# One transfer instead of two for each query and key tile of the first batch

## The chip, the cores and the metric

The kernel runs on 1 core of one Trainium2 chip. The metric is the device time of one execution in microseconds; lower is better. Three parts of that core matter here besides its matrix engine TensorE (PE): VectorE (DVE), ScalarE (ACT) and GpSimd (POOL), which do the elementwise work, SyncE (SP), whose queue issues almost every DMA, and the 16 DMA engines that carry out what it issues.

## What the kernel computes

Attention over `q`, `k`, `v` of shape 4 batches x 8 heads x 576 tokens x 64, then a dense layer with softplus, then a layer with one of eight experts per token.

```python
# attention: two parts, added
q_d = q.reshape(B, H, S // 4, 4, D).mean(axis=3)      # k_d, v_d alike
out_d = softmax_attention(q_d, k_d, v_d)               # 144 x 144 per head
mask = abs(pos[:, None] - pos[None, :]) < 4            # a band of 7 keys
out_local = softmax_attention(q, k, v, mask)
x = repeat(out_d, 4, axis=2) + out_local               # -> 2304 x 512
# dense layer
h = x @ w_in; g = softplus(h); x = g @ w_out           # 512 -> 2048 -> 512, weights in float64
# experts
e = argmax(x @ w_gate + modality_bias[id]); out = gate * (relu(x @ w1[e]) @ w2[e])
```

## The kernel before, in words

Attention works on pairs of heads: 16 pairs, four for each of four batches. The queue of work is a list of jobs. A `Down` job of a pair loads its queries, keys and values, brings queries and keys into the layout "two heads x 64 features on 128 partitions, tokens along the row" (`qT`, `kT`) and does the downsampled attention. Three `Local` jobs of the same pair do the band, 192 tokens each. Every job has six steps (`st_T`, `st_S`, `st_E`, `st_N`, `st_Ta`, `st_PV`), spread over successive steps of the queue (`pieces`), so that several jobs are under way at once. The first 19 steps of the queue run ahead of everything else; from then on the attention pieces are dealt out between the matrix products of the dense layer. At the same time the float64 weights of that layer are loaded (`raw`) and turned into float32 by DVE and ACT (`from_f64`, L439 to L443). The dense layer goes through six blocks of 384 tokens; block 0 needs the local attention of all four pairs of batch 0.

The tile framework fixes the order of the instructions on each engine when the program is built. It takes them in program order and by priority, against a timeline that it simulates, so an instruction whose assumed duration changes can move others.

The change touches how the first batch's queries and keys arrive. In batch 0 (`PE_TRANSPOSED = 1`) a tile `qr` or `kr` holds 96 partitions; partition p has tokens 6p to 6p+5 (`RT = 6`) of both heads. The tile of before is ordered token, head, feature, and each head is loaded by a DMA of its own (L135); what one DMA writes in a partition is six separate rows of 64 floats, 256 bytes each. `trans` (L162) then takes each of the six token slots, a block of 96 x 128 that holds both heads, through TensorE as a transposition against the identity (L172), three slots to a PSUM tile `pT`, and copies the PSUM tile to `qT` or `kT` with DVE or ACT (L177). Batches 1 to 3 use other loads (L139) and a transposition on DVE (L166), which the change leaves alone. On SP's queue each pair's loads stand in the order `qr`, `qr`, `kr`, `kr`, `vr` (L144), and `lv` (L291, values of the band) and `raw` (L456, L460) come between pairs. `qr` and `kr` of batch 0 share two buffers each (tags `wis`, `wos`), so the loads of pair 2 wait for the transpositions of pair 0.

The sums over four tokens (`sum4`, L188 and L185), the scores (L210, L311), the exponentials (L225, L325), the normalizing (L232, L331), the second transpositions (L239, L336) and the products with the values (L248, L344) follow from `qT` and `kT`. `warm` (L264) puts one idle product behind some steps.

Of the kernel before, what the change touches and what calls it, by code (L numbers as in the profile page):

```python
# [9 lines left out]
F32 = mybir.dt.float32  # L10
# [8 lines left out]
B, H, S, D = 4, 8, 576, 64  # L19
# [15 lines left out]
RT = 6  # L35
RP = S // RT
NBLK = S // 32
# [18 lines left out]
def band_attention__softplus_mlp__top1_moe(  # L56
# [14 lines left out]
    nc = tc.nc  # L71
    V, A, G, T = nc.vector, nc.scalar, nc.gpsimd, nc.tensor
# [8 lines left out]
    ident = const.tile([128, 128], F32, name="ident")  # L81
# [19 lines left out]
    mlp = ctx.enter_context(tc.tile_pool(name="mlp", bufs=2))  # L101
# [19 lines left out]
    class Down:  # L121
# [3 lines left out]
        def load(self):  # L125
            b, h0 = self.b, 2 * self.hp
            self.raw = []
            for src, nm in ((q, "qr"), (k, "kr")):
                tag = {"qr": "wis", "kr": "wos"}[nm] if b == 0 else "raw"
                on_pe = b < PE_TRANSPOSED  # L130
                t = mlp.tile([RP, RT, 2, D] if on_pe else [128, NBLK, 32], F32, tag=tag, name=nm,
                             bufs=RAWB if tag == "raw" else 2)
                for h in range(2):
                    if on_pe:
                        nc.sync.dma_start(out=t[:, :, h, :], in_=src[b, h0 + h].rearrange("(p r) d -> p r d", r=RT))  # L135
                        continue
                    for c in range(2):
                        p0 = h * D + c * 32
                        nc.sync.dma_start(  # L139
                            out=t[p0:p0 + 32],  # L140
                            in_=src[b, h0 + h, :, c * 32:(c + 1) * 32].rearrange("(n t) d -> t n d", t=32))
                self.raw.append(t)
            t = mlp.tile([SDH, 2, 2, FACTOR, D], F32, tag="raw", name="vr", bufs=RAWB)
            nc.sync.dma_start(  # L144
                out=t.rearrange("p h a r d -> p (h a) (r d)"),
                in_=v[b, h0:h0 + 2].rearrange("h (a p r) d -> p (h a) (r d)", a=2, p=SDH, r=FACTOR),
            )
            self.raw.append(t)
# [13 lines left out]
        def trans(self, i):  # L162

            t = apool.tile([128, S], F32, tag=("qT", "kT")[i], name="qkT", bufs=4)
            if self.b >= PE_TRANSPOSED:
                V.transpose(t, self.raw[i].rearrange("p n d -> p (n d)"))  # L166
                return t
            half = RT // 2
            for g in range(2):
                ps = pa("pT")  # L170
                for r in range(half):
                    T.transpose(ps[:, r * RP:(r + 1) * RP], self.raw[i][:, g * half + r].rearrange("p h d -> p (h d)"),  # L172
                                ident[:RP, :RP])
                warm(ps)
                o = t.rearrange("m (p r) -> m r p", r=RT)[:, g * half:(g + 1) * half, :]
                x = ps[:, :half * RP].rearrange("m (r p) -> m r p", r=half)
                (A.copy if i or g else V.tensor_copy)(o, x)  # L177
            return t
# [81 lines left out]
    def warm(ps):  # L260

        if 4 <= nloc[0] < 12:
            for i in range(1):
                T.matmul(ps[:, 384:384 + 128], ident, ident[:, :128], start=True, stop=True)  # L264

    def pa(name):

        if not started[0]:
            nps[0] += 1
            if nps[0] % 2:  # L270
                return psy.tile([128, 512], F32, tag="py", name=name)
        return psa.tile([128, 512], F32, tag="pa", name=name)
# [554 lines left out]
    if 0:  # L827
        ps = pa("pW")
# [169 lines left out]
    p, q, pos_q = stages[-1]  # L998
# [57 lines left out]
```

## Time and profile before

| | |
|---|---|
| median of 3 runs | 785.83 us (784.47 to 790.5) |
| the profiled execution's own time | 786.35 us |
| its span, first to last instruction | 784.5 us |
| PE busy | 749.1 us (95%) |
| DVE, ACT, POOL busy | 504.8, 461.2, 449.9 us |
| mean granted TensorE clock | 0.987 |

The profiled execution takes 1.85 us more than its span, and 0.52 us more than the median. The busy time of PE is nearly the whole span, but it is a mean over stages that differ: the early stages, where the change lies, have to be read by themselves.

### The profile page before, as it was taken

To read this page: it belongs to the slowest core of one execution; us is meant where nothing else is said; L and a number is where in the kernel's file an instruction comes from. 1 tells how busy PE (TensorE), PEld (TensorE's weight loads), DVE (VectorE), ACT (ScalarE), POOL (GpSimd) and SP (SyncE) were. 2 spreads that over 40 slices of the span, in tenths; PEclk is the share of its full clock that TensorE was granted. 3 is DMA by queue.
4 is the path that set the end of the run, shared out by engine and by line. 5 is a ranking of instruction groups with operands and counts; after the bars stand their busy time and mean duration, and the time that the engine had idled before them with its cause. 6 is when DMAs were issued, how large, how long until landed. Compare 5 with 4: busy or idle time off the path is not lost.

```text
span 784.5 us, 13833 instructions
## 1 busy us (share of the span) xinstructions
PE 749.1 (95%) x4917; PEld 657.3 (84%) x4918; DVE 504.8 (64%) x1067; ACT 461.2 (59%) x1204; POOL 449.9 (57%) x447
## 2 busy tenths in 40 slices
PE   6977999899999999999999999999999999999995
PEld 5754656579899989899899999999998889889884
DVE  6888999856764567976654555445996394274322
ACT  5835666667676646667565756555865365355432
POOL 3446322757765566766556556565769365455632
PEclk9987999999999999999999999999999999999999
DMA  8769666415000241311000100071002012001002
GB/s 190 175 138 270 194 196 188 77 26 119 23 13 15 71 83 28 72 24 52 1 13 13 52 1 2 1 271 65 1 21 101 21 61 82 0 1 68 14 0 85
DMA packets 111447, 55.46 MB, mean 71 GB/s; under 512 B 89593, under 2 KB 102411, under 8 KB 111371
## 3 DMA queue, kind: packets, MB, share of 16 engines
q1 hardware_dynamic: 111083, 53.98, 25.7%
q8 instruction: 41, 0.67, 0.4%
q10 hardware_dynamic: 288, 0.52, 0.2%
q14 instruction: 35, 0.29, 0.1%
HBM read 45.05 MB, written 9.44 MB: 69 GB/s over the span
## 4 chain that ended last, share of the span: by engine, by line
PE 75%; DVE 14%; DMA 3%; issue 2%; ACT 2%; SPq 2%; POOL 2%; DVEq 0%; ACTq 0%
PE py L623 22%; PE ph L582 20%; PE py L940 11%; PE ph L784 10%; DVE cva L442 2%; PE pS L311 2%; PE pO L344 2%; DMA qr<-in_q_dram 2%; PE ph L579 2%; DVE cva L440 2%; PE pA L336 2%; PE pS L210 1%; DVE cva L441 1%; PE pO L248 1%; DVE wi L443 1%
## 5 line engine op out<-in xcount | busy, mean ns | idle before, releaser
L623 PE MATMUL py<-g,wos 128*128 128x384 f32 x1056 | 212.5, 342 | 2.4 <-POOL g L606 1.1
L623 PEld LDWEIGHTS py<-g,wos 128*128 128x128 f32 x1056 | 181.7, 188 | 9.0 <-issue 3.0
L582 PE MATMUL ph<-xT,wis 128*128 128x384 f32 x960 | 183.1, 338 | 0.0
L582 PEld LDWEIGHTS ph<-xT,wis 128*128 128x128 f32 x960 | 166.6, 188 | 1.6 <-issue 0.4
L479 POOL TENSOR_TENSOR wis<-wi,wis 128x512 fp32r<-128x512 f32 x80 | 104.4, 1305 | 72.6 <-ACT wis L478 66.7
L479 POOL TENSOR_TENSOR wos<-wo,wos 128x512 fp32r<-128x512 f32 x88 | 117.8, 1339 | 47.5 <-ACT wos L478 47.4
L588 ACT ACTIVATE ga<-ph 128x384 f32<-128x384 f32 x96 | 46.9, 489 | 77.9 <-PE ph L582 74.9
L604 DVE SCALAR_TENSOR_TENSOR ph<-ph,ga 128x384 f32<-128x384 f32 x80 | 44.7, 560 | 49.4 <-ACT ga L590 49.4
L784 PE MATMUL ph<-xs,ws 128*128 128x384 f32 x378 | 73.9, 336 | 1.2 <-DVE u L789 1.2
L478 ACT CAST wos<-wo 128x512 fp32r<-128x512 f32 x88 | 54.3, 617 | 30.8 <-PE py L623 26.3
L784 PEld LDWEIGHTS ph<-xs,ws 128*128 128x128 f32 x378 | 67.1, 188 | 4.8 <-DVE u L789 1.6
L789 DVE TENSOR_TENSOR u<-ph,u 128x384 f32<-128x384 f32 x60 | 33.3, 555 | 58.6 <-PE ph L784 58.2
L940 PE MATMUL py<-wos,gs 128*128 128x512 f32 x270 | 69.0, 394 | 0.7 <-POOL gs L795 0.4
L325 ACT ACTIVATE ls<-ls,lst 128x70 f32<-128x70 f32 x144 | 49.4, 344 | 25.5 <-DVE lst L319 16.1
L940 PEld LDWEIGHTS py<-wos,gs 128*128 128x128 f32 x270 | 50.0, 188 | 9.9 <-POOL gs L795 0.8
L479 POOL TENSOR_TENSOR wos<-w2s,wos 128x512 fp32r<-128x512 f32 x24 | 33.5, 1395 | 34.3 <-ACT wos L478 34.3
L331 POOL TENSOR_TENSOR ls<-ls,lst 128x210 f32<-128x210 f32 x48 | 28.8, 601 | 42.2 <-DVE lst L330 15.5
L590 ACT ACTIVATE ga<-ga 128x384 f32<-128x384 f32 x96 | 50.2, 524 | 1.7
L589 ACT ACTIVATE ga<-ga 128x384 f32<-128x384 f32 x96 | 50.4, 525 | 0.4
L478 ACT CAST wis<-wi 128x512 fp32r<-128x512 f32 x80 | 48.9, 612 | 0.1
L579 PE MATMUL ph<-xN,wi 128*128 128x384 f32 x128 | 45.7, 499 | 1.2 <-DVE xf L360 1.1
L605 DVE CAST g<-ph 128x384 fp32r<-128x384 f32 x80 | 44.1, 552 | 4.2 <-PE py L623 1.1
(166 smaller groups left out, 1283.1 us busy)
## 6 DMA issues: line engine op xcount, KB each, us to landing
raw<-in_moe_w_in_dram SPq DMA_DIRECT2D x16, 512.0 KB
raw<-in_moe_w_out_dram SPq DMA_DIRECT2D x16, 512.0 KB
lv<-in_v_dram SPq DMA_DIRECT2D x72, 70.0 KB
vr<-in_v_dram SPq DMA_DIRECT2D x16, 288.0 KB
ydram<-y SPq DMA_DIRECT2D x12, 384.0 KB
yb<-ydram SPq DMA_DIRECT2D x12, 384.0 KB
out_dram<-ob SPq DMA_DIRECT2D x16, 256.0 KB
qr<-in_q_dram SPq DMA_DIRECT2D x48, 72.0 KB
```

The lines of the kernel that those rows point to most:

```text
L325: A.activation(s[:, i, :], s[:, i, :], AF.Exp, bias=st[:, 0, i], accum_out=st[:, 1, i])
L478: A.copy(w[:, 0], src)
L479: G.tensor_tensor(out=w[:, 1], in0=src, in1=w[:, 0].bitcast(F32), op=ALU.subtract)
L579: T.matmul(ps[:, :TB], wi[:, c, cc, :], xT[n][:, cc, :], start=(cc == 0), stop=(cc == CC - 1))
L582: T.matmul(ps[:, :TB], wt[:, w, cc, :], xT[n][:, x, cc, :], start=(i == 0), stop=(i == 3 * CC - 1))
L588: A.activation(a, ps[:, :TB], AF.Abs)
L589: A.activation(a, a, AF.Exp, scale=-1.0)
L590: A.activation(a, a, AF.Ln, bias=1.0)
L604: V.scalar_tensor_tensor(o, ps[:, :TB], 0.0, a, ALU.max, ALU.add)
L623: T.matmul(yps[n][dc][:, :TB], w[:, a, dsl], g[:, b, :], start=(c == 0 and i == 0), stop=(c == NC1 - 1 and i == 2))
L784: T.matmul(ps[:, :TB], ops[:, w, a, cc, :], xop[p, x][:, l, cc, :], start=i == 0, stop=i == 5)
L940: T.matmul(yps[n][t], g[:, a, t * 128:(t + 1) * 128], w[:, b, :], start=first and c == q and i == 0, stop=last and c == q + NQ and i == 2)
```

## The change

The tile becomes head, token, feature, so that the six tokens of one head are one row of 384 floats (1536 bytes) in a partition, both in memory and in the tile. One DMA brings both heads. A token slot's two heads no longer lie side by side in the tile, so each is transposed by a product of its own: 64 columns of weights, the 96 x 96 identity as the moving operand, results in partitions 0 to 63 for head 0 and 64 to 127 for head 1. Copies and everything behind them stay.

```diff
-                t = mlp.tile([RP, RT, 2, D] if on_pe else [128, NBLK, 32], F32, tag=tag, name=nm,
+                t = mlp.tile([RP, 2, RT, D] if on_pe else [128, NBLK, 32], F32, tag=tag, name=nm,
                              bufs=RAWB if tag == "raw" else 2)
-                for h in range(2):
-                    if on_pe:
-                        nc.sync.dma_start(out=t[:, :, h, :], in_=src[b, h0 + h].rearrange("(p r) d -> p r d", r=RT))
-                        continue
+                if on_pe:
+                    nc.sync.dma_start(out=t.rearrange("p h r d -> p h (r d)"),
+                                      in_=src[b, h0:h0 + 2].rearrange("h (p r) d -> p h (r d)", r=RT))
+                for h in range(0 if on_pe else 2):
                     for c in range(2):
...
                 for r in range(half):
-                    T.transpose(ps[:, r * RP:(r + 1) * RP], self.raw[i][:, g * half + r].rearrange("p h d -> p (h d)"),
-                                ident[:RP, :RP])
+                    for h in range(2):
+                        T.matmul(ps[h * D:(h + 1) * D, r * RP:(r + 1) * RP], self.raw[i][:, h, g * half + r, :],
+                                 ident[:RP, :RP], start=True, stop=True)
```

## Rows read from the trace of the kernel before

**Rows 1.** Busy us and instructions by engine, four stages, clock, DMA share, GB/s.

```profile
0.00:30.00 30.00, 21.83 (x164) 18.68 (x166) 21.42 (x46) 20.76 (x68) 11.21 (x35) 0.95 0.84 202
30.00:67.00 37.00, 26.71 (x279) 21.10 (x279) 31.30 (x74) 17.74 (x74) 16.90 (x21) 0.82 0.71 158
67.00:140.00 73.00, 70.10 (x404) 42.55 (x404) 72.62 (x158) 47.64 (x139) 28.65 (x28) 0.99 0.71 204
140.00:784.50 644.50, 630.45 (x4075) 574.95 (x4073) 379.48 (x792) 375.09 (x926) 393.13 (x364) 1.00 0.16 44
```

**Rows 2.** Chain of waits, first 15 us: start us, us, what.

```profile
4.88 3.84 DMA qr<-in_q_dram
...
10.03 4.31 DMA qr<-in_q_dram
```

**Rows 3.** Timeline of SP's queue, loads of pairs 0 and 1: start us, us.

```profile
0.78 1.41 SPq L135 DMA_DIRECT2D qr<-in_q_dram  x2
...
4.26 1.24 SPq L135 DMA_DIRECT2D qr<-in_q_dram  x2
```

**Rows 4.** Timeline of PE, transpositions of queries, pairs 0 and 3.

```profile
4.97 1.20 PE L172 MATMUL pT<-ident,qr 96*128 96x96 f32 x6 [4.97 <-DMA qr<-in_q_dram]
...
20.26 0.70 PE L172 MATMUL pT<-ident,qr 96*128 96x96 f32 x6
```

**Rows 5.** Line 135, issues of queries: ns min/median/max, first and last start.

```profile
L135 SPq DMA_DIRECT2D qr<-in_q_dram x8: 563/625/739, 0.8 to 14.1; - x8
```

**Rows 6.** DMA packets and queue share, first 7.4 to 9 us, then 520 to 530 us.

```profile
DMA packets 1422, 0.36 MB, mean 222 GB/s; under 512 B 1422, under 2 KB 1422, under 8 KB 1422
...
q1 hardware_dynamic: 1422, 0.36, 98.4%
...
DMA packets 1584, 3.60 MB, mean 360 GB/s; under 512 B 93, under 2 KB 93, under 8 KB 1582
...
q1 hardware_dynamic: 1582, 3.58, 100.3%
```

**Rows 7.** Busy by engine as in the first group, 10 to 30 us.

```profile
10.00:20.00 10.00, 9.08 (x60) 7.98 (x60) 8.69 (x16) 7.42 (x26) 2.64 (x5) 1.00 0.96 218
20.00:30.00 10.00, 9.21 (x89) 7.89 (x88) 8.34 (x23) 9.58 (x36) 4.27 (x8) 0.86 0.88 224
```

**Rows 8.** Timeline of PE: an ordinary product early, a product in column halves late.

```profile
15.78 1.73 PE L210 MATMUL pS<-dkT,dbd 128*96 128x144 f32 x6
...
201.84 0.57 PE L344 MATMUL pO<-laT,lv 70*64 70x64 f32 x12
```

**Rows 9.** Lines 172, 210 and 344: ns of one, min/median/max.

```profile
L172 PE MATMUL pT<-ident,qr x24: 246/367/395, 5.0 to 20.7; 96*128 96x96 f32 x24
...
L210 PE MATMUL pS<-dkT,dbd x96: 284/286/556, 10.5 to 385.4; 128*96 128x144 f32 x96
...
L344 PE MATMUL pO<-laT,lv x576: 222/222/369, 24.5 to 511.3; 70*64 70x64 f32 x192
```

**Rows 10.** Who waited for whom: us in total, times, longest; SP's queue last.

```profile
ACT cva L439 <- DMA raw<-in_moe_w_out_dram: 3.4, 1, 3.4
...
DVE cva L440 <- ACT cva L439: 2.7, 1, 2.7
...
SPq L291 <- PE pO L344: 3.8, 2, 2.4
```

**Rows 11.** DVE groups by line, 60 to 140 us: busy, mean ns, idle before.

```profile
L440 DVE TENSOR_SCALAR cva<-cva 128x512 f32<-128x512 f32 x26 | 14.1, 541 | 2.7 <-ACT cva L439 2.7
```

**Rows 12.** Timeline, a weight conversion alone and one beside GpSimd.

```profile
29.17 0.42 DVE L440 TENSOR_SCALAR cva<-cva 128x512 f32<-128x512 f32 x1
...
35.46 1.61 POOL L479 TENSOR_TENSOR wis<-wi,wis 128x512 fp32r<-128x512 f32 x1 [0.23 <-DMA vr<-in_v_dram]
...
35.85 1.50 DVE L440 TENSOR_SCALAR cva<-cva 128x512 f32<-128x512 f32 x1
```

**Rows 13.** Line 579, first products of the dense layer: ns min/median/max, first and last start.

```profile
L579 PE MATMUL ph<-xN,wi x128: 485/486/847, 66.9 to 172.0; 128*128 128x384 f32 x128
```

## Prediction

> **What bounds the kernel now.** I read the stages first, because a change in the first 25 us can't be judged from a mean over 784. After 140 us PE is the bound (630 of 644 us busy), from 67 to 140 us DVE is (72.6 of 73), and before that nobody is: in the first 30 us PE, DVE and ACT are each busy about 21 us, while the DMA engines are at 0.84 [rows 1]. So the opening is a stage of hand-offs, and the question is which one ends last. The chain of waits answers it: twice in the first 15 us it runs through a load of queries, 3.84 and 4.31 us from issue to landing [rows 2]. Ahead of each stands SP's queue, which issues without a pause: the two loads of a tile take 1.24 to 1.41 us [rows 3], 0.625 us for one at the median [rows 5]. The DMA engines are nearly full too, 0.96 from 10 to 20 us [rows 7]. So the first batch's data come as fast as SP can issue and the DMA engines can carry, and both are what the change lightens. But the compute engines are not far behind: from 10 to 30 us ACT is busy 17.0 of 20 us, DVE 17.0 and PE 18.3 [rows 7].
>
> **Issues.** Sixteen issues become eight. Each removed one is worth about 0.63 us of SP's queue [rows 5], 5.0 us in all, and 4.4 us for the seven tiles up to the queries of the last pair. That the remaining issue costs more because it describes both heads can't be seen before; its rows are fewer (192 against 576 per old DMA), so I take the old price, and the upper end is that it costs as much as the two, which makes this term nothing.
>
> **Transfers.** The bytes are the same; the rows become longer. A window in which only 256-byte rows move has 1422 packets in 1.6 us at a share of 98.4%: 1.6 x 16 x 0.984 / 1422 = 17.7 ns each. A window of long rows has 1582 packets of 2263 bytes on average in 10 us at 100.3%: 101.4 ns each [rows 6]. No row of this kernel is 1536 bytes long. On the line between the two it takes 17.7 + 1280 x 0.0417 = 71 ns (estimate). A tile is now 1152 packets, 72 for each DMA engine, 1.27 us; it will be 192, 12 for each, 0.85 us. That is 0.42 us a tile, 3.4 us for eight and 2.9 us for the seven. The bounds are nothing (1536 bytes at the rate of the short rows) and 0.44 us a tile (at the rate per byte of the long rows).
>
> **The first tile.** Its second load starts 0.78 us after its first (1.41 us for two, less 0.63). Without it, and with 0.42 us less to carry, the first transposition, now at 4.97 us [rows 4], starts near 3.8.
>
> **Transpositions.** 48 become 96, and so do the weight loads. Six of 96 columns take 1.20 us early on [rows 4]; less the last one's 395 ns [rows 9], that is a step of 161 ns, 1.68 ns a column, and 91 ns at 20.26 us, where TensorE had gone to the upper of its two levels (0.70 less 0.246, over five). The new ones have half the weight columns and the same 96 moving columns, so alone each would cost the same step again. But the two heads write different halves of the partitions. The product with the values does that already: twelve of 64 columns in 0.57 us [rows 8], a step of (570 - 222) / 11 = 32 ns [rows 9], where 64 columns in a row would take 61 at the rate of the transposition. So the halves run side by side and a pair costs one step. The price on PE is nothing to a few per cent; if they don't run side by side, it is 36 x 161 + 12 x 91 ns = 6.9 us over the opening.
>
> Is the transposition of before faster than an ordinary product, so that the change gives something up? The ordinary product of 144 columns takes 1.73 us for six [rows 8], a step of (1.73 - 0.556) / 5 = 0.235 us [rows 9] or 1.63 ns a column, against 1.68 for the transposition. There is nothing to give up. The Trainium skill speaks against the change here: "TensorEngine Tiling (Array Packing)", sections Key Properties and Performance Considerations, has column tiling exclude the transposing mode of float32 and has a switch of the tiling mode drain the engine. By the first, a step would be longer than before, which these rows do not bear out, since the kernel's transposition has the step of a product; by the second a switch would lengthen the group, and the twelve products, which lie between untiled ones, still show 32 ns a step.
>
> **What of it lies on the path.** At the last pair the queries come earlier by between 2.9 us (the DMA engines' saving) and 4.4 us (SP's). The engines behind them can't follow all the way: to finish the same work sooner they have to give up idle time, and from 10 to 30 us ACT and DVE have 3.0 us of it each, PE 1.7 [rows 7]; the earlier start adds 1.2. So the work that ends at 30 us ends earlier by 1.7 to 4.2 us, and I take 3.0, nearest to ACT's and DVE's idle time, since PE's busy share is modelled and its gaps are smaller than the row says. With the lower bounds of both terms it is 0.
>
> **Carrying it to the end.** From 30 to 67 us the chain changes hands between PE, DVE, SP and DMA. Two waits there could swallow the gain. SP waits 3.8 us for a buffer that PE's product with the values frees [rows 10]: that product comes earlier by the same amount. DVE waits 2.7 us for ACT, which waits 3.4 us for a load of `w_out` [rows 10]: the load stands in SP's queue behind the ones that are shortened. Neither hangs on something that the change leaves in its place, so the 3.0 us pass. From 67 us DVE, then PE, has no idle time in which it could be lost. The values (`vr`) and the copies to `qT` and `kT` keep their cost; of SP's queue the loads of batch 1 and the raw weights are moved ahead, into DMA engines that still have 0.71 to carry [rows 1].
>
> The sum against the profiled execution: 786.35 - 3.0 = 783.3 us. That execution lies 0.5 us above the median of 785.83, whose runs spread over 6.0 us, so I forecast **783.0**. The forecast's own range is 780.5 to 785.
>
> **Rivals.**
> - *Hidden anyway.* ACT and PE are the limit after all (9.58 and 9.21 of 10 us from 20 to 30 [rows 7]) and the wait for the raw load or for a buffer is met by something else: under 1 us of gain, 785 to 786.5.
> - *More than the idle time.* The opening up to 67 us is one queue of SP and DMA work, and what it is relieved of is gained whole: 5.0 us for SP, perhaps with the upper clock of TensorE reached earlier as its work gets denser: 778 to 781, in the extreme a little under.
> - *The order is dealt anew.* The build places instructions by a simulated timeline. Where a conversion of weights meets GpSimd it takes 1.50 us in place of 0.42 [rows 12]; in the bound stretch of DVE the mean is 541 ns over 26 [rows 11], so collisions cost there some 3 us on this line alone. Another order can have more or fewer: 3 to 9 us either way, 777 to 795.
> - *The halves don't run side by side* (slower). The place is PE from 4 to 20 us, at the lower level; the price is the 6.9 us above, of which the idle time of PE takes some; it decides once the step of one head is above about 80 ns. PE is then busy all the way, the gain is gone and 2 to 4 us are added: 788 to 790. Against it stand the twelve products in 0.57 us.
> - *The single DMA does not spread* (slower). If its pattern with the head in the middle put it on two DMA engines, a tile would take 192 x 71 ns / 2 = 6.8 us, eight in a row 54 us, and the opening would end some 30 us later, near 815. `vr` has the same form, head in the middle, and keeps the 16 busy at 0.96 together with the others [rows 7].
>
> **How the numbers follow.** Forecast 0.50, hidden 0.20, more 0.14 (0.06 of it under 778), new order 0.09 (a third each beyond 1% on either side), halves 0.05 (0.01 beyond 1%), no spread 0.02. One per cent, 7.9 us, is about what this measurement can tell from no change. Faster by more: 0.06 + 0.03, and 0.01 for the new order on top of "more", 0.10. Slower by more: 0.03 + 0.01 + 0.02, 0.06. The rest, 0.84, within. The range of 778 to 788.5 leaves out the end of "more" (0.06), most of the new order (0.06), the halves (0.04) and the spread (0.02).
>
> **What would show it.** The first transposition starts near 3.8 us and the last pair's queries 3 to 4 us earlier than 20.26. Line 135's successor shows eight issues of about 0.63 us. Twelve products in the place of six take about 1.2 us at the lower level; near 2.1 us the halves are serial. The DMA share from 10 to 20 us falls below 0.96. The first product of the dense layer, now at 66.9 us [rows 13], comes about 3 us earlier. The forecast is wrong if that start moves and the end does not, or if the conversions of weights between 60 and 140 us have another mean than 541 ns.

## The result, and the profile after

The changed kernel takes 798.43 us (median of 6 runs, 796.72 to 813.04) against 785.56 us for the kernel before (6 runs, 784.47 to 790.5): a ratio of 1.0147, 95% interval 1.0109 to 1.0185. It is slower by 1.5%; the forecast was 783.0, with 788.5 as the upper end of the range. Ratios, here and below, are taken from the fast runs alone (the run of 813.04 us is a slow one), so they are not the quotients of the medians given beside them. The profiled execution took 797.16 us, its span is 795.4 us where it was 784.5, so the trace holds 10.9 us of the loss. In the changed kernel the lines behind the loads carry numbers one higher (L173 for the transpositions, L444 and L580 for what was L443 and L579).

The stages first, as in [rows 1]: busy us and instructions of PE, PE's weight loads, DVE, ACT and POOL, then granted clock, DMA share and GB/s.

```profile
0.00:30.00 30.00, 20.73 (x210) 18.00 (x211) 22.40 (x38) 14.02 (x39) 9.65 (x28) 0.74 0.93 218
30.00:67.00 37.00, 33.06 (x327) 26.48 (x327) 22.38 (x57) 20.47 (x86) 13.79 (x22) 0.80 0.42 92
67.00:140.00 73.00, 67.72 (x378) 41.43 (x379) 71.92 (x165) 45.34 (x140) 32.28 (x32) 0.93 0.73 212
140.00:780.00 640.00, 631.32 (x4117) 575.50 (x4116) 389.08 (x805) 378.67 (x936) 395.04 (x365) 1.00 0.17 44
```

The place to look is the second row. From 30 to 67 us DVE is busy for 22.4 us, where it had 31.3, and the DMA share falls from 0.71 to 0.42. Work that DVE and the DMA engines did there before is missing, and nothing in the change took work from either in that stage. The granted clock of the first stage falls from 0.95 to 0.74; how far that column can be read there is said further down.

SP's timeline of the changed kernel shows what happened to the loads: start us, us, what.

```profile
0.78 0.40 SPq L134 DMA_DIRECT2D qr<-in_q_dram  x1
1.23 0.44 SPq L134 DMA_DIRECT2D kr<-in_k_dram  x1
...
11.22 0.41 SPq L457 DMA_DIRECT2D raw<-in_moe_w_in_dram  x1
11.73 1.88 SPq L134 DMA_DIRECT2D kr<-in_k_dram  x1
...
17.62 0.36 SPq L134 DMA_DIRECT2D qr<-in_q_dram  x1
...
26.27 0.44 SPq L134 DMA_DIRECT2D kr<-in_k_dram  x1
...
28.81 0.37 SPq L457 DMA_DIRECT2D raw<-in_moe_w_in_dram  x1
...
63.90 0.36 SPq L461 DMA_DIRECT2D raw<-in_moe_w_out_dram  x1
```

The same timeline of the kernel before, at loads that did not stand among the rows ahead of the prediction:

```profile
14.84 1.53 SPq L135 DMA_DIRECT2D kr<-in_k_dram  x2
...
36.92 0.47 SPq L456 DMA_DIRECT2D raw<-in_moe_w_in_dram  x1
...
56.29 0.36 SPq L460 DMA_DIRECT2D raw<-in_moe_w_out_dram  x1
56.74 0.39 SPq L456 DMA_DIRECT2D raw<-in_moe_w_in_dram  x1
57.22 0.45 SPq L460 DMA_DIRECT2D raw<-in_moe_w_out_dram  x1
```

SP spends less time on a tile, as forecast (0.40 and 0.44 us where two loads took 1.41 and 1.30). But the queue is no longer the same queue. The keys of pair 3, issued at 14.84 us before, are issued at 26.27, behind seven loads of batch 1, and those of pair 2 stand behind a raw weight load. And after 28.81 us no raw weights are asked for until 63.90, where before there were four such loads between 36 and 58 us. What SP stood at between, in the view of waits from 30 to 70 us (us in total, times, longest):

```profile
SPq L292 <- PE pO L345: 9.1, 2, 7.3
SPq L139 <- POOL vs L158: 8.7, 3, 7.3
SPq L144 <- DVE wi L444: 2.3, 1, 2.3
```

Twice it stood for 7.3 us at a load whose buffer was not yet free: once at band values, until PE's product with the values of an earlier job was done, and once at a load of a later batch, until GpSimd had summed the values of a pair behind batch 0 (L158 sums on GpSimd only from the fifth pair on). The raw weights were queued behind. The wait for `pO` was 3.8 us before [rows 10]. DVE meanwhile (waits from 40 to 67 us) went through the attention, step by step with its partners:

```profile
DVE ls L318 <- POOL ls L332: 2.9, 2, 2.1
DVE lst L330 <- ACT ls L326: 2.9, 3, 1.3
DVE dsm L231 <- ACT de L226: 1.9, 1, 1.9
DVE dmx L213 <- PE pS L211: 1.8, 1, 1.8
```

Before, the conversions of weights filled such gaps; in that stretch of the changed kernel there is none. They are made up later, and this is the row that gives the end: the last group of conversions (line, engine, operation, count, ns min/median/max, first and last start), here of the kernel before and of the one after.

```profile
L443 DVE SCALAR_TENSOR_TENSOR wo<-raw,cva x10: 675/691/966, 99.4 to 150.9; 128x512 int32<-128x512 int32 x10
```

```profile
L444 DVE SCALAR_TENSOR_TENSOR wo<-raw,cva x11: 673/682/1375, 104.1 to 159.9; 128x512 int32<-128x512 int32 x11
```

The last conversion starts 9.0 us later. From it to the end of the span it is 633.6 us before and 635.5 after, so 9.0 of the 10.9 us are lost by then. The first product of the dense layer, which had its start at 66.9 us [rows 13], starts at 76.0:

```profile
L580 PE MATMUL ph<-xN,wi x128: 485/486/847, 76.0 to 181.4; 128*128 128x384 f32 x128
```

The transpositions, in the timeline of PE after (the answer to [rows 4]), at the first tile of queries and at the keys of pairs 2 and 3:

```profile
4.27 2.19 PE L173 MATMUL pT<-ident,qr 96*64 96x96 f32 x24 [4.27 <-POOL mask L428]
...
19.74 1.23 PE L173 MATMUL pT<-ident,kr 96*64 96x96 f32 x12 [1.72 <-DMA kr<-in_k_dram]
...
36.43 1.23 PE L173 MATMUL pT<-ident,kr 96*64 96x96 f32 x12
```

Twelve products show as 24 instructions, and a tile takes 2.19 us instead of 1.20. The last keys are transposed at 36.4 us, where it was 22.75. For the first tile the view names a mask of GpSimd as what it waited for. The products read no mask, and the kernel with the products alone, whose masks are made at the same times (from 1.7 to 5.2 us), started earlier:

```profile
3.79 0.55 PE L242 MATMUL pT<-ident,qr 96*64 96x96 f32 x2 [3.79 <-POOL mask L497]
```

So a mask made behind that time is not needed to start, and the naming is doubtful; its load is the likelier reason, but the trace does not say so.

So two things changed, of which the diff shows only one: the instructions, and the order in which the build put all instructions. The experiments take them apart.

### The profile page after: what moved, and what is told of

It is laid out like the page before. It is cut to its first block, busy times and chain, and to the rows that moved or that the text cites. A ratio compares the mean times of both kernels' runs of the same rounds, so it can differ in the third digit from the quotient of the medians.

```text
span 795.4 us, 14109 instructions
## 1 busy us (share of the span) xinstructions
PE 760.3 (96%) x5061; PEld 667.1 (84%) x5062; DVE 509.4 (64%) x1067; ACT 462.4 (58%) x1204; POOL 452.9 (57%) x447
## 4 chain that ended last, share of the span: by engine, by line
PE 75%; DVE 14%; DMA 4%; issue 2%; POOL 2%; ACT 1%; SPq 1%; DVEq 0%; POOLq 0%; ACTq 0%
PE py L624 22%; PE ph L583 21%; PE py L941 11%; PE ph L785 10%; DVE cva L443 2%; PE pO L345 2%; PE pS L312 2%; PE pA L337 2%; DVE cva L441 2%; PE ph L580 2%; DMA raw<-in_moe_w_in_dram 2%; DVE wi L444 1%; DMA vr<-in_v_dram 1%; DVE wo L444 1%; PE pO L249 1%
## 5 line engine op out<-in xcount | busy, mean ns | idle before, releaser
L480 POOL TENSOR_TENSOR wis<-wi,wis 128x512 fp32r<-128x512 f32 x80 | 104.7, 1309 | 72.5 <-ACT wis L479 66.9
L332 POOL TENSOR_TENSOR ls<-ls,lst 128x210 f32<-128x210 f32 x48 | 30.8, 641 | 39.7 <-DVE lst L331 20.0
L580 PE MATMUL ph<-xN,wi 128*128 128x384 f32 x128 | 46.5, 506 | 1.8 <-DVE ls L318 1.1
```

The source lines that it names most:

```text
L480: G.tensor_tensor(out=w[:, 1], in0=src, in1=w[:, 0].bitcast(F32), op=ALU.subtract)
L580: T.matmul(ps[:, :TB], wi[:, c, cc, :], xT[n][:, cc, :], start=(cc == 0), stop=(cc == CC - 1))
```

## The experiments

Order is taken from the instructions by a function at the end of the program. It goes through a list of positions for each engine and adds, between neighbours, an edge that only the order in the queue has to respect, no semaphore. In outline:

```python
last = None
for at in want[engine]:
    if last is not None:
        tc.add_manual_dep(have[at], last.name, DependencyInfo(NoSync, DATA), reason="order")
    last = have[at]
```

**The changed kernel in the order of before.** All five engines take the order of the kernel before; where the change has two products for one transposition, both stand in its place.

```diff
+ORDER = ...      # every engine: the order of the kernel before
+    in_order(tc)
```

> The changed kernel, its instructions on every engine held in the order in which the kernel before has them (the two products of a token slot where its transposition stood, the one load where the second of the two stood). Theory 'order': the loss of 12 us comes from the order that the build chose anew, which puts two loads of keys behind raw weights and loads of the next batch; then this run takes 782 to 788 us. Theory 'price': the loss comes from the products, which keep TensorE 2.2 us a tile in place of 1.2, eight tiles at its lower level; then 793 to 799 us, about as much as the changed kernel. A mixture would land between, near 790.

784.98 us (10 runs) against 787.88 for the kernel before on the same chip (25 runs), ratio 0.9969, interval 0.9945 to 0.9993. The whole loss is gone, with every instruction of the change in place.

**The kernel before in the order of the changed one.** The same function, the other way round.

> The kernel before, two loads and six transpositions a tile, its instructions held in the order that the changed kernel has. Theory 'order': 794 to 800 us, the loss without the products. Theory 'price': 783 to 789 us, no loss without the products.

800.32 us (5 runs), ratio 1.0175, interval 1.0132 to 1.0218. The order alone, without a single changed instruction, costs about what the change costs. (No rows of its profile are read here.) With the two runs above and the changed kernel itself, the four corners are 1, 1.0147, 0.9969 and 1.0175: the order carries the loss, the instructions none. No run holds the kernel before to its own order, so a small effect of the added edges themselves is not measured; the two halves of the change below, held to that order, come out at 0.9986 and 0.9984.

**Products alone, order kept.** The tile and the two loads of before, the twelve products in place of six transpositions, in the order of before.

```diff
-                    T.transpose(ps[...], self.raw[i][:, g * half + r].rearrange("p h d -> p (h d)"), ident[:RP, :RP])
+                    for h in range(2):
+                        T.matmul(ps[h * D:(h + 1) * D, ...], self.raw[i][:, g * half + r, h, :], ident[:RP, :RP], ...)
```

> The products alone: the tile and its two loads as before, each head's half transposed by a product, in the order of the kernel before. Theory 'price': up to 8 x 1.0 us more on the path, 791 to 797 us. Theory 'order': the extra microsecond of a tile is mostly hidden under the wait for the next load, 785 to 789 us.

785.39 us (10 runs), ratio 0.9986, interval 0.9956 to 1.0016.

**One load alone, order kept.** The tile and the transpositions of before; one DMA brings both heads, rows of 256 bytes stay.

```diff
-                for h in range(2):
-                    if on_pe:
-                        nc.sync.dma_start(out=t[:, :, h, :], in_=src[b, h0 + h].rearrange("(p r) d -> p r d", r=RT))
...
+                if on_pe:
+                    nc.sync.dma_start(out=t, in_=src[b, h0:h0 + 2].rearrange("h (p r) d -> p r h d", r=RT))
...
```

> The single issue alone: one load for both heads, but into the old tile, so in rows of 256 bytes, and the transpositions as before, in the order of the kernel before. If SP's queue is what holds up the first batch, 781 to 784 us; if the DMA engines are, 785 to 787 us. Neither theory of the loss expects it above 788.

786.20 us (10 runs), ratio 0.9984, interval 0.9949 to 1.0018. By time neither half of the change differs from before. (The load alone lies in the range expected if the DMA engines are the limit, 785 to 787 us, but the kernel before takes 2.3 us more here than in the first comparison, so the two ranges are not told apart.) The start of the dense layer does differ between these kernels. It is, in turn, of the whole change, of the products alone and of the load alone, all in the order of before:

```profile
L649 PE MATMUL ph<-xN,wi x128: 485/486/847, 63.8 to 168.1; 128*128 128x384 f32 x128
```

```profile
L649 PE MATMUL ph<-xN,wi x128: 485/486/847, 64.4 to 169.3; 128*128 128x384 f32 x128
```

```profile
L647 PE MATMUL ph<-xN,wi x128: 485/486/847, 67.4 to 171.6; 128*128 128x384 f32 x128
```

With 66.9 us before [rows 13], the whole change shows the 3.1 us that I had forecast, but the products alone show 2.5 of them, and half the issues alone none. These are single profiles, and their spans differ by 2.3 us at most, while the runs of the kernel before beside these experiments lie between 782.78 and 791.0 us: the differences are a hint, no more. The stage view shows what goes with them. Four stretches of the whole change in the order of before, columns as above:

```profile
10.00:20.00 10.00, 9.20 (x128) 7.73 (x126) 7.92 (x15) 7.13 (x26) 2.63 (x5) 1.00 0.95 242
20.00:30.00 10.00, 9.75 (x129) 7.99 (x127) 9.00 (x23) 9.80 (x36) 4.64 (x8) 1.00 0.98 212
30.00:40.00 10.00, 8.59 (x101) 6.71 (x102) 9.89 (x25) 7.19 (x32) 6.02 (x4) 1.00 0.55 122
40.00:50.00 10.00, 9.84 (x122) 7.75 (x121) 9.93 (x22) 4.67 (x21) 5.26 (x9) 1.00 0.63 118
```

and the last two of them in the kernel before (the first two are [rows 7]):

```profile
30.00:40.00 10.00, 8.59 (x90) 6.71 (x89) 9.07 (x19) 6.52 (x26) 5.08 (x5) 0.97 0.61 136
40.00:50.00 10.00, 9.45 (x88) 7.46 (x89) 7.94 (x22) 4.13 (x17) 5.25 (x6) 0.83 0.58 114
```

The granted clock is 1.00 in all four where it was 0.86 from 20 to 30 and 0.83 from 40 to 50 us. PE was busy for about as long and issued more in it. The products alone also show 1.00 in these four stretches, the load alone 0.87 and 0.83 like the kernel before. In the next stretch, with less work on PE, the clock is the lower one. First the whole change in the order of before, then the kernel before:

```profile
50.00:60.00 10.00, 2.78 (x28) 2.19 (x29) 7.76 (x19) 4.00 (x16) 5.31 (x9) 0.57 0.93 250
```

```profile
50.00:60.00 10.00, 4.42 (x77) 3.56 (x77) 8.68 (x23) 3.53 (x16) 3.08 (x7) 0.89 0.75 169
```

Over the whole second stage, 30 to 67 us, both have 0.82. And in the first 20 us the column can't be read: it says 1.00 for the kernel before, whose transposition at 17.30 us still has the price of the lower level, while the one at 20.26 us has that of the upper (0.70 us [rows 4]):

```profile
17.30 1.17 PE L172 MATMUL pT<-ident,kr 96*128 96x96 f32 x6
```

By these durations, whole tiles are at the upper level from 14.66 us in the whole change (1.21 us a tile) and from 15.23 us in the products alone, both in the order of before, and in the load alone in that order not yet at 17.42 us. But the load alone in an order of its own (below), which has no such products, is there at 13.87 us (0.69 us a tile). So it is not shown that the gain comes from the clock, nor that the clock comes from the products.

**SP's order alone.** The changed kernel with SP in its own order and the other engines in that of before. SP and, below, PE are the two engines that were exchanged singly; DVE, ACT and GpSimd were not.

> The changed kernel; SP's queue in its own order (keys of pair 2 behind a load of raw weights, keys of pair 3 behind seven loads of the next batch), all other engines in the order of the kernel before. The loss has been seen to come with the order. Theory 'loads': it sits in SP's queue, because the late keys hold up every step of pairs 2 and 3; then 793 to 800 us. Theory 'engines': it sits in how DVE, ACT, POOL and PE interleave their work, and the queue alone costs little; then 783 to 789 us.

801.5 us (4 runs), ratio 1.0173, interval 1.0097 to 1.025. The order of the loads is enough for the whole loss.

**Loads moved forward.** If the late keys are what costs, moving them forward in the changed kernel's own order should cure it. In the first kernel the keys of pair 2 stand right behind their queries, and queries and keys of pair 3 ahead of the raw weights; in the second only the keys of pair 3 are moved, to right behind their queries.

> The changed kernel in its own order on every engine but for three loads in SP's queue: the keys of pair 2 go right behind its queries, the queries and keys of pair 3 right behind the values of the band that follow. Theory 'loads': the loss goes, 784 to 789 us. Theory 'engines': it stays, 794 to 800 us, because the other queues still have their order of work.

> The changed kernel in its own order but for one load: the keys of pair 3 go right behind its queries, at about 18 us in place of 26. Theory 'loads': this is most of it, since pair 3 ends last: 788 to 793 us. Theory 'engines': no effect, 795 to 800 us.

805.09 us (4 runs), ratio 1.0237, interval 1.0172 to 1.0301, and 799.37 us (4 runs), ratio 1.0163, interval 1.0118 to 1.0208. Neither cures anything; the first kernel is the slowest of all, beyond either expectation. The theory that the loads' place alone is the fault falls. The engines behind keep an order that was made for late keys: in the first kernel the keys of pair 3 are issued at 15.6 us and the last of them transposed at 38.4, in the changed kernel at 26.3 and 36.4.

**PE's order alone.** The changed kernel in the order of before, with only TensorE in the order of the changed kernel.

> The changed kernel with SP, DVE, ACT and GpSimd in the order of before and only TensorE in the order that the build dealt to the changed kernel. Theory 'a matching set' (each engine's order fits the others' of the same plan, and an engine held to another plan waits for them): 1.008 to 1.02 to before, the first dense product at 70 us or later. Theory 'the loads' order is what costs' (SP's queue alone carries the loss): 0.995 to 1.003, the first dense product near 64 us.

791.22 us (10 runs), ratio 1.0041, interval 1.0005 to 1.0077; the first dense product starts at 71.1 us. That is slower, with less than the 1.008 that a matching set was to cost at least, and the interval reaches down into the other theory's 0.995 to 1.003; the start of the dense layer fits the matching set (70 us or later against 64). Against the same instructions fully in the order of before (0.9969) it is 0.7%, measured on another chip. Of the two orders tried singly, SP's costs the more.

**Which edit deals a new order.** Four kernels take whatever order the build gives them: products with the old tile and loads; one load with short rows and transpositions; one product of 128 columns for each transposition; two loads of long rows with products.

> The products alone, with the old tile and its two loads, in the order that the build chooses for them. Its queue moves only the keys of pair 3, behind two loads of raw weights and one of the band's values, and the engines' work is dealt anew too. Theory 'loads': one load late by some 4 us, so 786 to 791 us. Theory 'engines': no statement from the loads; the order of the engines differs from that of before in its own way, 783 to 800 us.

> The tile and the transpositions of before, the two loads of a tile made one (rows of 256 bytes stay), in the order that the build deals. Its queue of loads has the keys of pairs 2 and 3 behind values and band values, as in the changed kernel, though ahead of batch 1. Theory 'any edit that the plan sees deals a new order, and early keys are what makes one good': 1.005 to 1.015. Theory 'only the dearer products on TensorE bring the slow order': 0.995 to 1.003.

> The tile and the two loads of before; each transposition made one product of 128 columns instead of two of 64, in the order that the build deals. That order stays near the one of before: only the keys of pair 3 fall behind values and band values. Theory 'products on TensorE are dearer, whatever the order': at least 1.005. Theory 'the order carries the loss, in proportion to how late the keys come': 0.998 to 1.008, the first dense product at 65 to 71 us.

> The tile of the changed kernel (whole rows of six tokens) and its 96 products of 64 columns, but each head loaded by a DMA of its own as before, in the order that the build deals. Only the keys of pair 3 come late in its queue of loads, the keys of pair 2 stand where they stood before. Theory 'late keys cost, each pair its part': 1.000 to 1.010, between before and the changed kernel. Theory 'products bring the slow order in any case': 1.010 to 1.020, like the changed kernel.

| kernel, order of its own | ratio | interval |
|---|---|---|
| products alone (797.31 us, 4 runs) | 1.0123 | 1.0085 to 1.0162 |
| one load, short rows (793.54 us, 10 runs) | 1.0073 | 1.0035 to 1.0112 |
| unsplit products (794.48 us, 10 runs) | 1.0092 | 1.0060 to 1.0124 |
| two loads of long rows, products (798.53 us, 4 runs) | 1.0146 | 1.0075 to 1.0218 |

All four are slower. The theory that only the dearer products bring a worse order falls with the second row: half the issues, nothing else, and 0.7% are gone, where the same instructions in the order of before cost nothing (0.9984). The theory that the price grows with how late SP's queue has the keys is not borne out by the last two: in both, only the keys of pair 3 come late, and they lose 0.9% and 1.5% where it allowed 0.8% and 1.0%; the lower ends of both intervals lie within that.

What orders these kernels (all but the kernel before in the order of the changed one) is the end of the weight conversions. In each of them a last row like the one above was read for the last start; spans are of the profiled executions, one of each kernel, so neighbours that differ by a few us may change places.

| kernel | span | first dense product | last conversion starts | from there to the end |
|---|---|---|---|---|
| whole change, order of before | 782.3 | 63.8 | 147.0 | 635.3 |
| products alone, order of before | 782.8 | 64.4 | 147.8 | 635.0 |
| before | 784.5 | 66.9 | 150.9 | 633.6 |
| one load alone, order of before | 784.6 | 67.4 | 150.6 | 634.0 |
| one load, own order | 788.1 | 68.9 | 154.1 | 634.0 |
| order of before, PE's own | 789.2 | 71.1 | 155.0 | 634.2 |
| unsplit products, own order | 791.0 | 73.2 | 156.7 | 634.3 |
| two long-row loads, own order | 791.7 | 70.9 | 156.7 | 635.0 |
| after | 795.4 | 76.0 | 159.9 | 635.5 |
| after, keys of pair 3 moved | 795.9 | 76.5 | 161.2 | 634.7 |
| products alone, own order | 798.8 | 76.3 | 163.4 | 635.4 |
| order of before, SP's own | 799.7 | 80.7 | 166.2 | 633.5 |
| after, three loads moved | 803.6 | 84.2 | 168.1 | 635.5 |

Spans differ by 21.3 us and the last column by 2.0. Everything that any of these edits did to the time had happened when DVE began its last conversion; what follows is the same stretch of work of PE for all of them. And DVE has too little slack to make up for a late start. In the slowest kernel it was busy for 20.41 of 30, 17.95 of 37 and 68.94 of 73 us in the three stages, 107.3 us up to 140, in the fastest 21.26, 34.58 and 72.62, together 128.5. The difference, 21.2 us, is the difference of the spans (21.3); for each of the other eleven, too, what DVE lacks up to 140 us and what the span is longer, both against the fastest, agree within 1.7 us. The rows are:

```profile
30.00:67.00 37.00, 27.88 (x289) 21.24 (x289) 34.58 (x82) 19.93 (x87) 19.53 (x24) 0.82 0.73 164
```

for the whole change in the order of before, and for the changed kernel with three loads moved:

```profile
30.00:67.00 37.00, 31.92 (x239) 25.01 (x238) 17.95 (x45) 19.01 (x76) 13.86 (x19) 0.60 0.32 61
```

The second row also has the lower clock, 0.60 against 0.82. How much of the loss goes through PE's clock and how much through the waits of SP and DVE is not taken apart here. The two loads of long rows with products do not decide it: their granted clock reads 1.00 in the first 30 us and 0.86 to 67, against 0.95 and 0.82 before, and still DVE is busy for only 27.15 us in the second stage and the span is 7.2 us longer; but at 17.37 us a tile of queries takes 2.19 us there, the price of the lower level, and from 30 to 40 us the clock is 0.50 where it was 0.97.

## Why the prediction was wrong

**The step that failed** is a term that the sum leaves out, the price of a new order. *Carrying it to the end* takes the queues as they were ("of SP's queue the loads of batch 1 and the raw weights are moved ahead") and lets the 3.0 us pass. The raw weights moved back: none was asked for between 28.81 and 63.90 us, and the order alone, on unchanged instructions, costs 1.75%. The text did name this, in the rival *The order is dealt anew*, with a chance of 0.09 and a reach of 3 to 9 us either way, up to 795. It is what happened, with 10.9 us of span and 798.43. The rival's mechanism was another one, though: its price was taken from collisions of conversions with GpSimd on DVE [rows 11, 12]. The same line's mean over that stretch, 541 ns before, is now

```profile
L441 DVE TENSOR_SCALAR cva<-cva 128x512 f32<-128x512 f32 x23 | 12.6, 550 | 0.9 <-ACT cva L440 0.9
```

550 ns: on this line collisions did not change. What a new order can cost here is DVE standing idle in the stage from 30 to 67 us, because SP's queue holds raw weights behind loads that wait for buffers. That stage was in the rows: 5.7 us of idle DVE before [rows 1], 14.6 after. *Carrying it to the end* saw two waits there and asked only whether 3 us pass through them. It did not ask what they cost when the queue is another one.

**The chance** was too small, and there was a reason to take it higher. The text says that the build places instructions by a simulated timeline. The change replaces 48 instructions and removes eight, all at the head of the program. Of the five edits that were built in an order of their own (the change and the four kernels above) all five came out slower, by 0.7 to 1.5%.

**Issues:** right in kind, too small in size. The remaining issue is not as dear as an old one (0.63 us) but 0.36 to 0.45 us, save one of keys that took 1.88 us, in a stretch where the DMA share is 1.03 (10 to 20 us).

**Transfers:** a window of the changed kernel from 2 to 4 us, in which nearly all packets are long rows, gives 2 x 16 x 0.881 / 378 = 74.6 ns for 1,430 bytes each:

```profile
DMA packets 378, 0.54 MB, mean 272 GB/s; under 512 B 22, under 2 KB 378, under 8 KB 378
...
q1 hardware_dynamic: 378, 0.54, 88.1%
```

The estimate was 71 ns for 1,536 bytes. That term stood.

**First tile:** forecast 3.8, measured 4.27 us, in one profile. What it waited for is not shown (see above).

**Transpositions:** the price was wrong, and so was the proof. Early on, 24 instructions of 64 columns take 2.19 us, a step of (2.19 - 0.367) / 23 = 79 ns; unsplit, 12 instructions of 128 columns take 2.77 us, (2.77 - 0.42) / 11 = 214 ns:

```profile
7.71 2.77 PE L172 MATMUL pT<-ident,kr 96*128 96x96 f32 x12
```

So a pair of halves costs 158 ns, less than an unsplit instruction, which speaks for some overlap of the halves. But a product of float32 is two instructions in these traces and a transposition is one. For a token slot that is 4 x 79 = 316 ns where the transposition took 161. At the upper level, in the changed kernel with the order of before, it is

```profile
14.66 1.21 PE L242 MATMUL pT<-ident,qr 96*64 96x96 f32 x24
```

1.21 against 0.70 us a tile [rows 4]. The price is 1.0 us a tile early and 0.5 later; 2.19 us is what the prediction had named as the sign of serial halves (near 2.1). The kernel before showed it, too. The products of scores in [rows 8] are marked x6 for three products, so the step of 0.235 us is half a product; I took it for a whole one and found 1.63 ns a column against 1.68. The products with the values there are marked x12 for six, so a product of 64 columns took 64 ns and not 32, no less than the 61 ns at the rate of the transposition: the row that was to show the halves side by side does not show it. With the first of these readings I set the Trainium skill aside. It says in "TensorEngine Tiling (Array Packing)", section Restrictions, that column tiling disables the transposing mode for float32. No run here asks for that mode on half the columns, so the rule itself is not tested; the change did give the mode up, for products, and the runs put about a factor of two on that (316 against 161 ns a slot). With the order kept, the time shows no cost of it: the products alone come out at 0.9986, interval 0.9956 to 1.0016. PE had idle time for it; in the first 10 us it is busy for 3.54 us before and 5.77 us with the products.

**Path gain:** 3.0 us forecast; with the order kept, 3.1 at the first dense product and 2.2 at the span (784.5 to 782.3), in one profile each. The size agrees; the path of the forecast does not. The queries of the last pair are issued earlier by 3.2 us, first the kernel before, then the whole change in the order of before:

```profile
13.51 1.24 SPq L135 DMA_DIRECT2D qr<-in_q_dram  x2
```

```profile
10.32 0.31 SPq L203 DMA_DIRECT2D qr<-in_q_dram  x1
```

But they are transposed at 19.60 us instead of 20.26 [rows 4], not 3 to 4 us earlier, and the keys of that pair at 23.12 instead of 22.75:

```profile
19.60 1.21 PE L242 MATMUL pT<-ident,qr 96*64 96x96 f32 x24
```

So the loads were not what the last pair waited for, and what there is of a gain arises behind it. Fewer issues alone gave 67.4 instead of 66.9, and products alone 64.4, which points at PE's work, the term that I priced at nothing; with single profiles that stays a guess.

**The other rivals:** the single load did spread (the DMA share is 0.93 in the first 30 us). Of *The halves don't run side by side* the price came, 2.19 us a tile, by another mechanism (two instructions a product), and the time that it forecast did not: with the order kept nothing is lost. "Hidden anyway" is not ruled out. With the order kept the dense layer starts earlier in one profile, but the interval of the time, 0.9945 to 0.9993, takes in a part of what that rival allowed (under 1 us of gain, a ratio above 0.9987).

**Open:** why the build's timeline arrives at orders that take longer on the chip; its own times were not compared with the chip's here. Also open is how DVE's idle time divides between late loads and PE's clock. The result for the change itself: held to the order of before, it runs at 0.9969 of the kernel before, the lowest ratio of the kernels run here, though its gain of 0.3% is hardly more than the interval's half width of 0.24%.

## What to carry to other kernels

Where a planner orders the instructions at build time, a small edit is two changes, and its own cost has to be measured with the old order pinned. Before forecasting such an edit, look for the queue that carries two streams (here SP, with attention's loads ahead of the weights) and for the engine that feeds the final bound (here DVE's conversions), and price a new order by the idle time that it can put there. When a product replaces a transposition, compare the number of instructions that the trace marks with the number of products in the code before taking a step between marks for the price of one.

## What was not expected of the hardware

- A float32 product shows as two instructions and a float32 transposition as one: x24 for 12 products, x12 for six unsplit ones, x6 for six transpositions. Unsplit products are the slowest form, 2.77 us a tile early against 2.19 split in halves and 1.20 transposed.
- The time of an issue on SP's queue went with the rows more than with the bytes, but not in proportion. One DMA of both heads in 1,152 rows of 256 bytes took 0.74 us at the first tile (one head's 576 rows 0.63 at the median), the same 288 KB in 192 rows of 1,536 bytes 0.40; one head's 96 rows of 1,536 bytes took no less, 0.44 (0.88 for two):

```profile
0.78 0.74 SPq L203 DMA_DIRECT2D qr<-in_q_dram  x1
```

- Rows are not all of it: the first load of values, which no edit touched, took 0.65 us before, 0.46 in the changed kernel and 1.38 with the single load of short rows.
- With the order kept, more instructions on PE from 20 to 50 us went with a higher granted clock (1.00 for 0.86, 0.97 and 0.83), and fewer from 50 to 60 us (28 for 77) with a lower one (0.57 for 0.89). That is no rule: in its own order the changed kernel has more instructions in the first 30 us (210 for 164) and the lower clock (0.74 for 0.95).
